# Second half of a fused attention and feed-forward kernel: the scheduler's order against program order on three engines

## The chip, the core and the metric

The kernel runs on one core of a Trainium2 chip. The core has a matrix engine (TensorE, here PE, with its weight loads shown apart as PEld), a vector engine (VectorE, DVE), an engine for functions of one element (ScalarE, ACT), a general engine (GpSimd, POOL) and SyncE (SP), which here only issues transfers. Each works through its own list of instructions in the order in which the built program holds it, and they meet through semaphores. The metric is the device time of the whole program in microseconds (us).

## The reference, cut to what matters

```python
attn = softmax(mask(q @ k.T / 8)) @ v            # 4 x 8 heads, 768 positions, window 128 and 4 sinks
x  = attn.reshape(3072, 512)
h  = np.maximum(x @ w_in, 0.0)                   # 512 -> 2048
x1 = h * h @ w_out                               # 2048 -> 512
a, b = x1 @ w1, x1 @ w2                          # 512 -> 1024, twice
out = (a * b @ w3) @ w_out2                      # 1024 -> 1024 -> 512, float32
```

## The kernel before, in words

The first half computes attention and the first feed-forward layer and writes most of `x1` to memory. Then `w3` and `w_out2` are folded into one matrix `w34` (`fold_T`, `fold_M`, L1193). What is left is the second half, on which the change works: per block of 512 tokens (six blocks, `order`, the loop after `pend = None`, L1555) and per slice `f` of 128 of the 1024 columns (eight slices), 48 passes in all. Every number is held as two float16 parts, high and low, so that one product is three matmuls for each of the two halves of its depth.

A pass is `ffn_C(n, f)` (L1291) and `ffn_D` (L1342). `ffn_C` gets `a` and `b` with a Strassen-like scheme: seven products of six matmuls each (128x128 weights, 256 columns), called P0 to P6 here after the first number in `prod(bx, 0, 0, True)`. They add up in three PSUM banks `bx`, `by`, `bz` (tile `cps`), taken in turn from four banks, so that the `by` of a pass is the `bx` of the pass before. Between the products of one bank stands a copy by ACT: s1 after P0, u2 after P4 (both into tile `cp`), u3 after P5 (tile `cq`). P4 may start when s1 is read, P5 when u2 is, P2 when u3 is. DVE adds c11 (tile `cq`, from s1 and P1), c22 (tile `cr`, from u3 and P3), c12 (tile `cr`, from u2 and P6), and multiplies twice into tile `asb`: s[0] after P2, s[1] after c12. Then `asb` is split into `h`: high part on ACT, low part on DVE. `ffn_D` is twelve matmuls of 512 columns with `h` as weights into four banks (tile `ops`), three for each bank; these run one pass behind, by `pend`.

Beside the passes stand: `upper` (ACT, tile `upj`), which sums squares for a range check, of each `h` and of some weights; `x1_ops` (L1251), which in a block prepares the operands `x1T` of the next one, with four subtractions on DVE (tile `x1t`) and seven splits, high part on ACT and low on DVE; `x1_load`, 1 MB from memory into `x1s`; and `ffn_out` (L1354), which at the end of a block reads the four `ops` banks, two on ACT and two on DVE, into `ost`, and sends it out, at the end of the program in four parts from SP and ACT by turns. `verdict` (L988) brings all range checks together on DVE into one number, which a one-column matmul `vps` sums and DVE turns into `flag`; every engine reads `flag` at the end and jumps over `general_path`, which does not run here.

Who sets the order: PE, ACT and DVE are wrapped in `InOrder` (L278). While `pinned[0]` is true, their instructions keep the order in which the code issues them. Otherwise a scheduler, which plans with times of its own, picks the order of each engine's list when the kernel is built. `pinned[0]` is true for most of the first half (L1488) and false from the last block of the first layer on, the second half included.

Of the kernel before, what the change touches and what calls it, by code (L numbers as in the profile page):

```python
# [14 lines left out]
ALU = mybir.AluOpType  # L15
# [281 lines left out]
def kernel(  # L297
# [17 lines left out]
    pinned = [False]  # L315
# [5 lines left out]
    KD, KF, K2 = DM // 128, DFF // 128, DF2 // 128  # L321
    BT = 512
    NB = NT // BT
    TB = BT // 128
# [41 lines left out]
    with ExitStack() as fast:  # L366
# [157 lines left out]
        def act_copy(out, in_, scale=1.0):  # L524
            ACT.activation(out=out, in_=in_, func=ACTF.Copy, scale=scale)
# [432 lines left out]
        def within(checks, name):  # L958

            n = sum(t.shape[1] * (t.shape[2] if len(t.shape) == 3 else 1) for t, _, _ in checks)  # L960
            inb = slab("t2", [128, n], F32, "inb", bufs=T2B)
            c0 = 0
            for t, bound, op in checks:
                n = t.shape[1] * (t.shape[2] if len(t.shape) == 3 else 1)
                d = inb[:, c0:c0 + n]
                if len(t.shape) == 3:
                    d = d.rearrange("p (a b) -> p a b", b=t.shape[2])
                DVE.tensor_scalar(out=d, in0=t, scalar1=bound, scalar2=None, op0=op)
                c0 += n
            low = top.tile([128, 1], F32, name=name)  # L970
            DVE.tensor_reduce(out=low, in_=inb[:, 0:c0], op=ALU.min, axis=AX.X)
            return low
# [12 lines left out]
            DVE.tensor_tensor(out=b, in0=b, in1=a, op=ALU.min)  # L985
            return b

        def verdict(low_att):  # L988

            low = within(  # L990
                ((st_w, W_MOST, ALU.is_lt), (st_w, W_LEAST, ALU.is_ge), (st_g, G_MOST, ALU.is_le)), "low_w"
            )
            up = within(((st_up, UP_MOST, ALU.is_le),), "low_up")
            DVE.tensor_tensor(out=low, in0=low, in1=up, op=ALU.min)
            DVE.tensor_tensor(out=low, in0=low, in1=low_att, op=ALU.min)

            DVE.scalar_tensor_tensor(out=low, in0=low, scalar=-1.0, in1=badf, op0=ALU.mult, op1=ALU.add)
            DVE.tensor_scalar(out=low, in0=low, scalar1=1.0, scalar2=None, op0=ALU.add)
            ps = bank("s0", "vps")
            PE.matmul(out=ps[0:1, 0:1], lhsT=low, rhs=ones, start=True, stop=True)  # L1000
            DVE.tensor_scalar(out=flag[0:1], in0=ps[0:1, 0:1], scalar1=0.5, scalar2=None, op0=ALU.is_ge)
# [289 lines left out]
        def ffn_C(n, f):  # L1291
# [23 lines left out]
            def add(out, a, ps):  # L1315
                DVE.tensor_tensor(out=out, in0=a, in1=ps, op=ALU.add)
# [3 lines left out]

            prod(bx, 0, 0, True)
            act_copy(s1, bx)
            prod(by, 3, 3, True)
            prod(bx, 4, 4, False)
            act_copy(u2, bx)
            prod(bz, 1, 1, True)
            add(c11, s1, bz)
            prod(bx, 5, 5, False)
            act_copy(u3, bx)
            add(c22, u3, by)  # L1330
# [4 lines left out]
            add(c12, u2, by)  # L1335
            mul(s[:, 1], c12, c22)
            h = slab("g", [128, 2, BT], F16, "h", bufs=GB)
            split(s.rearrange("p t c -> p (t c)"), h[:, 0], h[:, 1])
            h_t[n, f] = h
            yield  # L1340

        def ffn_D(n, f):  # L1342
            if f == 0:
                o_t[n] = [bank(f"b{c}", "ops") for c in range(TB)]
            h = h_t.pop((n, f))
            w = w34_t[f // 2]
            for t in range(TB):
                for i, (hp, wp) in enumerate(((0, 0), (0, 1), (1, 0))):
                    PE.matmul(
                        out=o_t[n][t], lhsT=h[:, hp, t * 128:(t + 1) * 128], rhs=w[:, wp, f % 2, :],  # L1350
                        start=(f == 0 and i == 0), stop=(f == K2 - 1 and i == 2),
                    )

        def ffn_out(n, k, last):  # L1354
            st = late_p[0].tile([128, TB, DM], F32, tag="ost", name="ost")
# [197 lines left out]
        rest = [w[0][:, c:d].rearrange("p a c f -> p (a c f)") for w in w12_t.values() for c, d in ((0, 4), (4, 7))]  # L1553
        rest += [w[:, 0].rearrange("p c f -> p (c f)") for w in w34_t.values()]
        pend = None  # L1555
        for o, n in enumerate(order):
            todo = []
            for f in range(K2):
                c = ffn_C(n, f)
                next(c)  # L1560
                if pend is not None:
                    ffn_D(*pend)
                next(c)
                if pend is not None and pend[1] == K2 - 1:
                    ffn_out(pend[0], o - 1, False)
                pend = (n, f)
                if f < 4:
                    upper(x1_t[n][0][:, 2 * f:min(7, 2 * f + 2)].rearrange("p a c f -> p (a c f)"))
                elif rest:
                    upper(rest.pop())  # L1570
                upper(h_t[n, f][:, 0])
                if f == 0 and o >= 1 and o + 1 < NB:
                    x1_load(o + 1)
                if f == 1 and o + 1 < NB:
                    x = x1s_t[o + 1]
                    todo = x1_ops(o + 1, x[:, 0:2], x[:, 2:4])
                for _ in range(2):
                    if todo:
                        todo.pop(0)()
        ffn_D(*pend)  # L1580
        assert not rest and ups[0] == NUP
        verdict(low_att)
        ffn_out(pend[0], NB - 1, True)

    gen = nc.values_load(flag[0:1, 0:1], min_val=0, max_val=1)
# [32 lines left out]
```

## Time and profile before

| what | us |
|---|---|
| three timed runs | 1108.42, 1110.32, 1110.94; median 1110.32 |
| the profiled execution, its own time | 1110.19 |
| its span on the core | 1108.0 |
| PE busy in the span | 1045.3 (94%) |
| DVE, ACT busy | 750.3 (68%), 709.4 (64%) |
| second half, first `cps` matmul to the end | 743.6 to 1108.0 |

Times in the trace count from the start of the span. A row of the timeline gives start, length, engine, operation, tile written and tiles read, and how many in a row; in brackets the idle time of the engine before it and what ended it. A PE row lasts until its last matmul's result is there, so rows that follow without a gap overlap by about 0.16.

### The profile page before, as it was taken

Reading aid. Unit: us, or ns where it says so; the run is one execution under the profiler, and the core shown is the slowest. Engines: PE = TensorE matmul, PEld = TensorE weight load, DVE = VectorE, ACT = ScalarE, POOL = GpSimd, SP = SyncE. Lnnn points to the kernel's source line nnn. Section 1 sums busy time; section 2 is a strip of 40 time slices with the busy share of each in tenths; the row PEclk is TensorE's granted clock in tenths of the full one; section 3 lists DMA queues with packets and bytes.
Section 4 is the critical chain, followed back from the end, with each engine's and each line's share of the span. In section 5 each row is a group of like instructions: output and inputs, shape, how many; then the busy total and the mean of one; then the engine's idle time right before and its main releaser. Section 6 shows DMA issues by size and latency. Waiting matters only on the chain. (4 is left out here: it accounts for less than half of the span.)

```text
span 1108.0 us, 20449 instructions
## 1 busy us (share of the span) xinstructions
PE 1045.3 (94%) x7146; PEld 636.4 (57%) x7146; DVE 750.3 (68%) x2292; ACT 709.4 (64%) x1836; POOL 45.0 (4%) x163
## 2 busy tenths in 40 slices
PE   6777897999999999999999998999999999999996
PEld 5665443555555555555554444457767776777774
DVE  8797888887788888877865667945363636453433
ACT  6975688887667666766754877854464546454532
POOL 2110111000000000000000000000000000000000
PEclk9867999999999999999999999999999999999998
DMA  8876787786567657556833324421020201010101
GB/s 189 157 157 140 179 204 184 150 183 122 104 144 145 117 107 173 118 114 144 147 68 99 115 96 140 164 75 40 2 77 1 77 1 39 1 39 1 38 1 41
DMA packets 265535, 113.46 MB, mean 102 GB/s; under 512 B 237648, under 2 KB 254032, under 8 KB 264784
## 3 DMA queue, kind: packets, MB, share of 16 engines
q1 hardware_dynamic: 265136, 111.55, 43.7%
q8 instruction: 58, 0.95, 0.4%
q14 instruction: 53, 0.43, 0.2%
q10 hardware_dynamic: 288, 0.52, 0.1%
HBM read 62.08 MB, written 11.53 MB: 66 GB/s over the span
## 5 line engine op out<-in xcount | busy, mean ns | idle before, releaser
L288 PE MATMUL hps<-xT,wi 128*128 128x512 f16 x1152 | 270.9, 386 | 0.0
L288 PE MATMUL x1ps<-g,wo 128*128 128x512 f16 x1152 | 265.6, 380 | 3.0 <-ACT g L288 2.0
L288 PE MATMUL cps<-x1T,w 128*128 128x256 f16 x2016 | 231.5, 273 | 7.2 <-DVE cq L288 4.6
L288 PEld LDWEIGHTS <-w 128*128 128x128 f16 x2016 | 196.9, 98 | 44.5 <-issue 9.1
L288 PEld LDWEIGHTS <-wi 128*128 128x128 f16 x1152 | 115.0, 100 | 123.2 <-issue 8.6
L288 PEld LDWEIGHTS <-wo 128*128 128x128 f16 x1152 | 109.8, 98 | 122.6 <-issue 5.7
L288 PE MATMUL ops<-w,h 128*128 128x512 f16 x576 | 133.5, 379 | 1.8 <-ACT h L288 1.8
L288 ACT ACTIVATE cp<-cps 128x256 f32<-128x256 f32 x96 | 36.1, 376 | 131.3 <-PE cps L288 131.3
L288 ACT ACTIVATE r<-hps 128x512 f32<-128x512 f32 x96 | 56.8, 592 | 94.7 <-PE hps L288 94.7
L288 ACT ACTIVATE pr<-pr,stt 128x264 f32<-128x264 f32 (+1 forms) x176 | 77.6, 483 | 32.9 <-DVE stt L288 31.5
L288 PEld LDWEIGHTS <-h 128*128 128x128 f16 x576 | 56.2, 98 | 58.1 <-ACT h L288 2.1
L288 DVE TENSOR_TENSOR ph<-pr,ph 128x512 f16<-128x512 f32 (+2 forms) x148 | 59.2, 436 | 35.2 <-ACT ph L288 33.2
L288 DVE SCALAR_TENSOR_TENSOR asb<-cq,cps 128x256 f32<-128x256 f32 x48 | 20.2, 420 | 87.6 <-PE cps L288 87.6
L288 DVE CUSTOM_DVE_ANT_0 pr<-sc,mask 128x264 f32<-128x264 f32 (+1 forms) x176 | 65.2, 400 | 16.1 <-PE sc L288 15.5
L288 PEld LDWEIGHTS <-pt 128*128 128x128 f16 x956 | 40.3, 98 | 34.5 <-issue 17.1
L288 ACT ACTIVATE ph<-pr 128x512 f16<-128x512 f32 (+2 forms) x148 | 55.9, 421 | 5.8 <-DMA pt<-ph 3.4
L288 ACT ACTIVATE g<-r 128x512 f16<-128x512 f32 x88 | 55.3, 629 | 2.4
L288 DVE TENSOR_TENSOR g<-r,g 128x512 f16<-128x512 f32 x56 | 38.6, 689 | 24.6 <-ACT g L288 24.4
L97 DVE SCALAR_TENSOR_TENSOR cvy<-cvy,cvt 128x512 int32<-128x512 int32 x72 | 49.1, 688 | 8.5 <-ACT cvy L86 8.3
L288 PE MATMUL y<-vp,pt 128*128 128x65 f16 (+1 forms) x888 | 40.6, 195 | 14.7 <-DVE xn L288 14.6
L288 DVE TENSOR_TENSOR h<-asb,h 128x512 f16<-128x512 f32 x48 | 33.2, 691 | 28.2 <-ACT h L288 28.2
L288 PEld LDWEIGHTS <-qT 128*128 128x128 f16 x592 | 41.4, 99 | 18.9 <-issue 0.7
(193 smaller groups left out, 1490.3 us busy)
## 6 DMA issues: line engine op xcount, KB each, us to landing
raw<-in_moe_w_out_dram SPq DMA_DIRECT2D x24, 512.0 KB
raw<-in_moe_w_dram SPq DMA_DIRECT2D x24, 512.0 KB
raw<-in_moe_w_in_dram SPq DMA_DIRECT2D x16, 512.0 KB
raw<-in_k_dram SPq DMA_DIRECT2D x84, 64.0 KB
raw<-in_q_dram SPq DMA_DIRECT2D x84, 64.0 KB
raw<-in_v_dram SPq DMA_DIRECT2D x84, 64.0 KB
x_dr<-x1e SPq DMA_DIRECT2D x20, 256.0 KB
x1s<-x_dr SPq DMA_DIRECT2D x5, 1024.0 KB
```

The source lines that it names most:

```text
L97: nc.vector.scalar_tensor_tensor(out=dst, in0=y, scalar=3, in1=t, op0=ALU.logical_shift_left, op1=ALU.bitwise_or)
L288: r = f(*args, **kw)
```

## The change

`pinned[0]` is set true ahead of the second half, so that PE, ACT and DVE run it as the code is written; SP isn't wrapped and is still planned. The code is written in another order for that. `ffn_C` hands over at two more places, after s1 and after c11, and the split of `asb` into `h` becomes a step of its own, `ffn_h`. A pass is now: P0, s1; split of the last pass's `h`; P3, P4, u2, P1, c11; `upper` of that `h`; P5, u3, c22; `ffn_D` of the last pass and, behind the last slice of a block, `ffn_out`; the load, two steps of `x1_ops`, the other `upper`; P2, s[0], P6, c12, s[1]. The last `ffn_D` may take the low parts of all four banks last (`i_outer`). The part of `verdict` that needs only old sums, with `low_att`, goes ahead of the last split as `verdict_w`.

```diff
+        def verdict_w(low_att):
             low = within(
                 ((st_w, W_MOST, ALU.is_lt), (st_w, W_LEAST, ALU.is_ge), (st_g, G_MOST, ALU.is_le)), "low_w"
             )
+            DVE.tensor_tensor(out=low, in0=low, in1=low_att, op=ALU.min)
+            return low
+
+        def verdict(low):
+
             up = within(((st_up, UP_MOST, ALU.is_le),), "low_up")
             DVE.tensor_tensor(out=low, in0=low, in1=up, op=ALU.min)
-            DVE.tensor_tensor(out=low, in0=low, in1=low_att, op=ALU.min)
...
             prod(bx, 0, 0, True)
             act_copy(s1, bx)
+            yield
             prod(by, 3, 3, True)
...
             add(c11, s1, bz)
+            yield
             prod(bx, 5, 5, False)
...
             h = slab("g", [128, 2, BT], F16, "h", bufs=GB)
-            split(s.rearrange("p t c -> p (t c)"), h[:, 0], h[:, 1])
+            h_t[n, f] = h, s.rearrange("p t c -> p (t c)")
+            yield
+
+        def ffn_h(n, f):
+            h, s = h_t[n, f]
+            split(s, h[:, 0], h[:, 1])
             h_t[n, f] = h
-            yield
-
-        def ffn_D(n, f):
+
+        def ffn_D(n, f, i_outer=False):
...
+            ti = [(t, i) for t in range(TB) for i in range(3)]
+            for t, i in sorted(ti, key=lambda x: x[1] == 2) if i_outer else ti:
...
         pend = None
+        pinned[0] = True
...
                 next(c)
                 if pend is not None:
+                    ffn_h(*pend)
+                next(c)
+                if pend is not None:
+                    upper(h_t[pend][:, 0])
+                next(c)
+                if pend is not None:
                     ffn_D(*pend)
...
+        low_w = verdict_w(low_att)
+        ffn_h(*pend)
+        upper(h_t[pend][:, 0])
+        ffn_D(*pend, i_outer=True)
+        assert ups[0] == NUP
+        verdict(low_w)
         ffn_out(pend[0], NB - 1, True)
```

PE, one pass in the middle of the first block, first matmul of each product alone (`x1T0` is the token operand, `cps_10185`, `cps_10186`, `cps_10187` are `bx`, `by`, `bz` of the pass, `cps_10105` and `cps_10106` those of the pass before it, `cps_10265` the next pass's `bx`; `ops` is `ffn_D`). Before:

```order
L288 MATMUL cps_10265<-x1T0_9374,w120_9039 128x256 [waits DVE_49]
...
L288 MATMUL cps_10105<-x1T0_9374,w12_7821 128x256 [waits Activation_49]
...
L288 MATMUL cps_10106<-x1T0_9374,w12_7821 128x256 [waits DVE_49]
...
L288 MATMUL cps_10185<-x1T0_9374,w120_8850 128x256 [waits Activation_49]
...
L288 MATMUL cps_10186<-x1T0_9374,w120_8850 128x256 [waits DVE_49]
...
L288 MATMUL cps_10187<-x1T0_9374,w120_8850 128x256 [waits DVE_49]
...
L288 MATMUL cps_10185<-x1T0_9374,w120_8850 128x256 [waits Activation_49]
...
L288 MATMUL ops_9977<-w34_9602,h_10174 128x512
```

These are P0 of the next pass, P2 and P6 of the last one, then P4, P3, P1, P5 of the pass, then `ffn_D`. The same pass now, whose banks are `cps_10181` to `cps_10183`:

```order
L288 MATMUL cps_10181<-x1T0_9374,w120_8850 128x256
...
L288 MATMUL cps_10182<-x1T0_9374,w120_8850 128x256 [waits DVE_49]
...
L288 MATMUL cps_10181<-x1T0_9374,w120_8850 128x256 [waits Activation_49]
...
L288 MATMUL cps_10183<-x1T0_9374,w120_8850 128x256 [waits DVE_49]
...
L288 MATMUL cps_10181<-x1T0_9374,w120_8850 128x256 [waits Activation_49]
...
L288 MATMUL ops_9977<-w34_9602,h_10180 128x512
...
L288 MATMUL cps_10181<-x1T0_9374,w120_8850 128x256 [waits Activation_49]
...
L288 MATMUL cps_10182<-x1T0_9374,w120_8850 128x256 [waits DVE_49]
```

That is P0, P3, P4, P1, P5, `ffn_D`, P2, P6: P0 has moved from a whole pass ahead to the head of its own pass, and one product instead of two stands between P4 and P5.

ACT, from the end of the first block's last whole pass on (`x1T0_10657` is the high part of the next block's operands). Before, and then the rows on the same operands now (`x1T0_9993`, prepared in the first block):

```order
L288 ACTIVATE cq_10421<-cps_10417 128x256
L288 ACTIVATE cp_10496<-cps_10493 128x256
L288 ACTIVATE x1T0_10657<-x1s_10575 128x512 x3
L288 ACTIVATE x1T0_10657<-x1t_10659 128x512 x2
L288 ACTIVATE x1T0_10657<-x1t_10660 128x512 x2
L288 ACTIVATE cp_10496<-cps_10493 128x256
```

```order
L288 ACTIVATE cq_10105<-cps_10101 128x256
L288 ACTIVATE x1T0_9993<-x1t_9995 128x512 x2
L288 ACTIVATE upj_10163,st_up_66<-x1T0_9374 128x512
L288 ACTIVATE cp_10184<-cps_10181 128x256
L288 ACTIVATE h_10180<-asb_10107 128x512
L288 ACTIVATE cp_10184<-cps_10181 128x256
```

Seven splits in a row between two copies have become one or two a pass, behind u3, with an `upper` behind them; and the split of `h` now stands between s1 and u2.

DVE, the end of the program, before and now:

```order
L288 TENSOR_REDUCE low_w_13687<-inb_13683 128x1
L288 SCALAR_TENSOR_TENSOR asb_13603<-cr_13602 128x256
L288 TENSOR_TENSOR h_13666<-asb_13603,h_13666 128x512
...
L288 TENSOR_SCALAR ost_13700<-ops_13186 128x512
L288 TENSOR_SCALAR ost_13700<-ops_13188 128x512
L288 TENSOR_SCALAR flag_63<-vps_13697 1x1
```

```order
L288 SCALAR_TENSOR_TENSOR asb_13599<-cr_13598 128x256
...
L288 TENSOR_REDUCE low_w_13671<-inb_13667 128x1
L288 TENSOR_TENSOR low_w_13671<-low_w_13671,low_att_8582 128x1
L288 TENSOR_TENSOR h_13666<-asb_13599,h_13666 128x512
...
L288 TENSOR_SCALAR flag_63<-vps_13697 1x1
L288 TENSOR_SCALAR ost_13700<-ops_13186 128x512
L288 TENSOR_SCALAR ost_13700<-ops_13188 128x512
```

The reduce has moved behind s[1], and `flag` ahead of the two reads of `ops`. On ACT the rows at the same place were `ost`, `ost`, two transfers, and are now by turns:

```order
L288 ACTIVATE ost_13700<-ops_13185 128x512
L288 DMA out_0_dram<-ost_13700 128x512
L288 ACTIVATE ost_13700<-ops_13187,cons_67 128x512
```

The first of these transfers sends what DVE writes into `ost`.

## Rows read from the trace of the kernel before

**Rows 1.** One stretch: length, then busy PE, PEld, DVE, ACT, POOL; clock; DMA.

```profile
991.10:1094.80 103.70, 103.70 (x776) 75.57 (x774) 40.43 (x90) 43.61 (x110) 0.00 (x0) 1.00 0.05 17
```

**Rows 2.** Timeline of PE: two groups of `ffn_D`, twelve passes apart.

```profile
998.29 2.75 PE L288 MATMUL ops<-w,h 128*128 128x512 f16 x12
...
1084.39 2.75 PE L288 MATMUL ops<-w,h 128*128 128x512 f16 x12
```

**Rows 3.** Timelines of PE, ACT and DVE at the end of the first block.

```profile
800.31 4.09 PE L288 MATMUL cps<-x1T,w 128*128 128x256 f16 x36
805.55 0.82 PE L288 MATMUL cps<-x1T,w 128*128 128x256 f16 x6 [1.14 <-DVE cq L288]
806.54 0.82 PE L288 MATMUL cps<-x1T,w 128*128 128x256 f16 x6 [0.18 <-ACT cp L288]
...
802.48 1.67 ACT L288 ACTIVATE x1T<-x1s 128x512 f16<-128x512 f32 x3 [3.14 <-PE cps L288]
...
803.28 1.89 DVE L288 TENSOR_TENSOR x1T<-x1s,x1T 128x512 f16<-128x512 f32 x3
805.08 0.41 DVE L288 TENSOR_TENSOR cq<-cp,cps 128x256 f32<-128x256 f32 x1
```

**Rows 4.** Instructions on the tile `cps`: shortest, median and longest, in ns.

```profile
L288 PE MATMUL cps<-x1T,w x2016: 269/273/273, 743.6 to 1094.7; 128*128 128x256 f16 x184
L288 ACT ACTIVATE cp<-cps x96: 359/378/385, 746.5 to 1089.1; 128x256 f32<-128x256 f32 x96
```

**Rows 5.** Timelines of PE and ACT: two hand-overs from PE through ACT to PE.

```profile
763.78 5.40 PE L288 MATMUL cps<-x1T,w 128*128 128x256 f16 x48
764.64 0.38 ACT L288 ACTIVATE cq<-cps 128x256 f32<-128x256 f32 x1 [2.47 <-PE cps L288]
...
746.53 0.37 ACT L288 ACTIVATE cp<-cps 128x256 f32<-128x256 f32 x1
746.95 0.81 PE L288 MATMUL cps<-x1T,w 128*128 128x256 f16 x6 [1.22 <-ACT cp L288]
```

**Rows 6.** Timelines of DVE and ACT in a pass without stall: s[1] and split.

```profile
795.76 0.42 DVE L288 SCALAR_TENSOR_TENSOR asb<-cr 128x256 f32<-128x256 f32 x1
796.24 0.62 ACT L288 ACTIVATE h<-asb 128x512 f16<-128x512 f32 x1
```

**Rows 7.** Groups of the second half: busy time, mean ns of one.

```profile
L288 DVE TENSOR_TENSOR x1t<-x1s 128x512 f32<-128x512 f32 x10 | 6.7, 686 | 3.5 <-DMA x1s<-x_dr 3.5
```

**Rows 8.** Timelines of PE, ACT and DVE where the second half begins.

```profile
735.41 8.37 PE L288 MATMUL w34ps<-wo,w3T 128*128 128x512 f16 x38
743.61 2.13 PE L288 MATMUL cps<-x1T,w 128*128 128x256 f16 x18
...
745.54 0.57 ACT L288 ACTIVATE w<-w34ps 128x512 f16<-128x512 f32 x1
...
748.26 0.68 DVE L288 SCALAR_TENSOR_TENSOR w<-w34ps,w 128x512 f16<-128x512 f32 x1
```

**Rows 9.** Timelines of PE, ACT and DVE at the end of the program.

```profile
1093.50 1.48 PE L288 MATMUL cps<-x1T,w 128*128 128x256 f16 x12
1096.80 2.76 PE L288 MATMUL ops<-w,h 128*128 128x512 f16 x12 [1.82 <-ACT h L288]
...
1096.12 0.63 ACT L288 ACTIVATE h<-asb 128x512 f16<-128x512 f32 x1 [4.62 <-DVE asb L288]
1099.90 0.94 ACTq L288 DMA_DIRECT2D out_dram<-ost  x2
...
1095.36 0.40 DVE L288 TENSOR_REDUCE low_w<-inb 128x1 f32<-128x240 f32 x1
1099.17 1.29 DVE L288 TENSOR_SCALAR ost<-ops 128x512 f32<-128x512 f32 x2 [0.34 <-PE ops L288]
1100.38 0.14 DVE L288 TENSOR_SCALAR flag<-vps 1x1 int32<-1x1 f32 x1
```

**Rows 10.** Queue instructions on the jump over `general_path`: count, ns, first start.

```profile
L1586 PEldq COMPARE_BRANCH x1: 4132/4132/4132, 1101.7 to 1101.7; - x1
```

More of the change, by code (lines that the diff above doesn't have):

```diff
@@ L986, in att_verdict @@
             return b
-        def verdict(low_att):
+        def verdict_w(low_att):
             low = within(
@@ L1346, in ffn_D @@
             w = w34_t[f // 2]
[L1347 to L1352, printed above, removed]
+            ti = [(t, i) for t in range(TB) for i in range(3)]
+            for t, i in sorted(ti, key=lambda x: x[1] == 2) if i_outer else ti:
+                hp, wp = ((0, 0), (0, 1), (1, 0))[i]
+                PE.matmul(
+                    out=o_t[n][t], lhsT=h[:, hp, t * 128:(t + 1) * 128], rhs=w[:, wp, f % 2, :],
+                    start=(f == 0 and i == 0), stop=(f == K2 - 1 and i == 2),
+                )
         def ffn_out(n, k, last):
@@ L1561 @@
                 if pend is not None:
-                    ffn_D(*pend)
[L1563 to L1571, printed above, removed]
+                    ffn_h(*pend)
[4 more added lines that the diff above has]
+                if pend is not None:
+                    ffn_D(*pend)
+                    if pend[1] == K2 - 1:
+                        ffn_out(pend[0], o - 1, False)
                 if f == 0 and o >= 1 and o + 1 < NB:
@@ L1579 @@
                         todo.pop(0)()
-        ffn_D(*pend)
-        assert not rest and ups[0] == NUP
-        verdict(low_att)
+                if f < 4:
+                    upper(x1_t[n][0][:, 2 * f:min(7, 2 * f + 2)].rearrange("p a c f -> p (a c f)"))
+                elif rest:
+                    upper(rest.pop())
+                next(c)
+                pend = (n, f)
+        assert not rest
+        low_w = verdict_w(low_att)
[4 more added lines that the diff above has]
+        verdict(low_w)
         ffn_out(pend[0], NB - 1, True)
```

## The prediction

> **What bounds the kernel now.** I read the stretches first. From 991 to 1095 us PE is busy for 103.70 of 103.70 us at a granted clock of 1.00, the full 2.4 GHz, while DVE and ACT are busy for some 40% of it [rows 1]: in the second half PE is the bound, and the two others matter only where they make it wait. So the question is how much of this half PE doesn't spend on issuing matmuls, and where.
>
> The length of a pass without a stall comes from two groups of ffn_D twelve passes apart: (1084.39 - 998.29) / 12 = 7.175 us [rows 2]. Forty-eight of them are 344.40 us. The half runs from its first matmul at 743.61 [rows 8] until the last matmul of the last ffn_D is issued. That group starts at 1096.80 and lasts 2.76, of which the last 0.16 is the way of the result into PSUM (a matmul of 256 columns lasts 0.273 and the next starts 0.109 after it, since 48 of them take 5.40 [rows 4, 5]): 1099.39. So the half takes 355.78 us, and 355.78 - 344.40 = **11.38 us are lost**. No order of the same matmuls gives back more than that.
>
> The loss stands in three places, in the timelines:
> - At block ends. ACT runs the seven splits for the next block in one go from 802.48, DVE follows with the low parts, and c11 comes after three of these, at 805.08 [rows 3]. PE has issued its 36 matmuls by 800.31 + 36 x 0.109 = 804.24 and goes on at 805.55, then again only at 806.54 instead of 806.21: 1.31 + 0.33, some 1.65 us. The pattern stands four times in the trace, so 6.6 us.
> - At the end: P6 is issued by 1093.50 + 1.48 - 0.16 = 1094.82, the last ffn_D starts at 1096.80, waiting for h [rows 9]: 1.98 us.
> - The rest, 11.38 - 6.6 - 1.98 = 2.8 us, at the beginning, where ACT splits operands of the second block before it serves the first products: w34's last part is read by ACT at 745.54, and DVE is done with it at 748.26 + 0.68 [rows 8].
>
> **The change part by part.**
>
> *The pass.* The work is the same; only the order differs. PE now runs P0, P3, P4, P1, P5, ffn_D, P2, P6. The hand-over s1 (P0 to P4) has one product, P3, as cover, where it had a whole pass; u2 (P4 to P5) has one, P1, where it had two; u3 (P5 to P2) has ffn_D. All depends on whether one product of 0.655 us (6 x 0.109) is enough. Counted from the start of the product's last matmul: 0.273 until it ends, some 0.04 until ACT starts (the sixth matmul of the run at 763.78 starts at 764.33, ends at 764.60, ACT starts at 764.64), 0.376 for the copy, 0.05 until PE goes on (copy over at 746.90, PE at 746.95): 0.74 us [rows 4, 5]. The cover, from the same point, is 0.109 + 0.655 = 0.764. That leaves 0.02 us. It is thin, but the trace shows this very case: the 48 matmuls from 763.78 hold P5, one product, P2, with the copy u3 between at 764.64, and 48 matmuls at 0.109 plus the tail make 5.40, what the row has. So no gap. I cost the hand-overs at 0, with 0.02 each as the upper end: two a pass, 95 of them, +1.9 us.
>
> What ACT does between them has to fit as well. With the end of P6 as zero, c12 and s[1] follow on DVE at 0.19 and 0.65; the split starts 0.48 after s[1] does, at 1.13, and takes 0.62 [rows 6], to 1.76. u2 is wanted at 3 x 0.655 + 0.19 = 2.16: 0.40 spare. The low part is ready at some 2.5, ffn_D wants it after P5 at 3.28. So a split between s1 and u2 costs nothing, as long as DVE isn't late.
>
> *Block ends.* The seven splits are spread over four passes, two in each, behind u3, where ffn_D covers them: two of 0.6 and an upper of 1.2 after u3, about 2.9 us after ffn_D's start, while the next s1 is wanted at 2.59 + 3 x 0.655 + 0.19 = 4.75. The 6.6 us go. In the one pass that has the four subtractions DVE is the tight engine: c22 ends about 1.0 after ffn_D's start, four subtractions and one low part of 0.69 each [rows 7] end at 4.4 (if none overlaps its neighbour) or 4.1 (two reads of ops take 1.29 together, so 0.6 from one to the next [rows 9]); then s[0] takes 0.42, and the next P3 may overwrite its bank at 4.6 to 4.9, and wants to at 4.555. That is 0.03 to 0.3 in each of five blocks; I take 0.05, so 0.25, with 0.1 and 1.5 as ends. ffn_out at a block's end reads the banks as they finish; the next ffn_D comes 7 products later, 4.6 us, so it hides. The loads on SP are issued a block ahead of use, and in the order now they still are.
>
> *Beginning.* P0 starts at 743.61 as before; P3 needs the bank of the last w34 product, which ends at 743.78. ACT, idle then, reads it by 744.4, DVE by 745.13 (0.57 and 0.68, [rows 8]), P3 at 745.18 where PE was free at 744.27: 0.91 stall. In the first pass there is no ffn_D, so P2 waits for u3 in full, 0.63. Together 1.54 instead of 2.8.
>
> *End.* The h of the last pass waits for c12, s[1] and the split as before. The reduce of 0.40 stood between c12 and s[1] [rows 9] and is now behind: 0.2 less (0 to 0.4), so 1.79 instead of 1.98. The last ffn_D had its low parts last already, so i_outer changes nothing.
>
> *Tail, from the last matmul to the end, 8.6 us.* flag no longer waits for DVE's two reads (1.29), so it is there 0.6 earlier; these reads come 0.6 later; and on ACT the second read now stands behind a transfer that waits for DVE's first one, so ACT reaches its own flag load some 0.65 later (its two transfers began at 1099.90 [rows 9]). The output's bytes end at about the same time, being held by bandwidth. Bounds -0.6 and +0.65; I take +0.3, since the later engine decides more of it. What ends the tail the rows leave open, the output's landing or the jump over general_path, which on PE lasts 4.13 us [rows 10].
>
> *The sum.* Lost now: 1.54 + 1.79 + 0.25 = 3.58, against 11.38: 7.80 us less; tail +0.3: 7.5 less. The profiled execution took 1110.19, the median is 1110.32, so they stand for each other: **1102.7 us**.
>
> **The rivals.**
> - *The hand-overs fall a little short.* Two a pass with 0.02 spare by modelled matmul ends. At 0.05 missing each, 95 x 0.05 = 4.8 us: 1107.5. For it: the longest copy is 0.385, and each wait now comes last. Against it: the run of 48 without a gap, which comes back in other blocks.
> - *They fall well short, slower than before.* The same place, s1 and u2, if PE's start after a wait that is really open costs more than rows show, say because ACT is held by the split of h whenever DVE is late. From 7.5 / 95 = 0.08 us each all is given back, from 0.1 it is slower; at 0.15 each, 14.3 us: 1117. Against it: the 0.40 spare above, and DVE's low load [rows 1].
> - *The stall at block ends changes its form.* If DVE's burst in one pass a block holds P3, and through s[1] the split and u2, for the 1.65 us that the old burst cost, 5 x 1.65 replace 6.6, and only beginning and end gain: 11.38 - 3.33 - 8.25 = -0.2, with the tail's 0.3 it is 0.5 more than before: 1110.7. Against it: 0.3 is the most that the durations make of it.
>
> - *The tail follows each engine's own jump.* If an engine needs some 4 us for the jump whatever the output does, ACT, the latest, sets the end: tail +0.65 instead of +0.3, 1103.0. PE's 4.13 us [rows 10] speak for it; that the output's landing isn't told apart from it in the rows, against. The Trainium skill (Runtime: NRT & Kernel Launch, section Instruction fetch mechanics) has this rule: a taken branch whose target isn't loaded stalls until its code is fetched. The length of PE's row agrees with it.
>
> **How the numbers follow.** The forecast gets 0.48, and the tail by the jump, which differs from it by 0.3 alone, 0.30, together 0.78; hand-overs a little short 0.12 (of it 0.02 so near that no change can be told); block ends in another form 0.04; well short 0.06. A measurement can tell about 0.2%, 2.2 us, from no change: the forecast, the tail's rival and most of the first rival lie below 1108.1, so faster 0.88; same 0.06; slower 0.06. Range: downwards burst and tail at their low ends give 1102.7 - 0.15 - 0.9 = 1101.7, and the runs of before reach 1.9 below their median, so 1100.3. Upwards burst 1.25, tail 0.35 and hand-overs 1.9 more: 1106.2.
>
> **What would show it.** PE's timeline of the second half as groups of 42 and 12 with no idle time behind ACT or DVE at block ends; ffn_D every 7.175 us; one gap of 0.9 before P3 at about 744.3 and one of 0.5 to 0.6 before P2 at 748; the last ffn_D starting near 1089, and the span ending near 1100.5. Wrong if the copies into cp show up as releasers of PE in every pass, or ffn_D comes later than 7.2 us after the last.

## The result and the profile after

The changed kernel takes 1099.4 us, median of four runs (1099.13 to 1101.41); the kernel before 1110.63 beside it. The ratio is 0.9899, 95% interval 0.9868 to 0.9929: faster by 11.2 us, and 3.3 below the predicted 1102.7. Direction and the mechanism of the second half are as predicted; the tail went the other way, and the time lies 0.9 under the range.

The profiled execution took 1101.41 at a span of 1099.2. The page, whose columns are busy time, share of the span and instructions, shows the same number of instructions as before on every engine. The span falls by 8.8, PE's busy time by 5.8, and DVE's rises by 7.9.

```profile
span 1099.2 us, 20433 instructions
...
PE 1039.5 (95%) x7146; PEld 635.0 (58%) x7146; DVE 758.2 (69%) x2292; ACT 711.0 (65%) x1836; POOL 47.9 (4%) x163
```

What [rows 1] showed for one good stretch now holds for nearly all of the second half. The view by stretches of after (length, busy PE, PEld, DVE, ACT, POOL, clock, DMA):

```profile
820.30:1086.00 265.70, 265.70 (x2003) 195.70 (x2001) 132.17 (x267) 133.03 (x321) 0.00 (x0) 1.00 0.07 25
```

PE's timeline of after at three places, the beginning, the end of the first block and the end of the program (start, length, engine, operation, count, and in brackets the idle time ahead and what ended it):

```profile
743.59 0.82 PE L288 MATMUL cps<-x1T,w 128*128 128x256 f16 x6
745.17 2.78 PE L288 MATMUL cps<-x1T,w 128*128 128x256 f16 x24 [0.76 <-DVE w L288]
748.42 4.74 PE L288 MATMUL cps<-x1T,w 128*128 128x256 f16 x42 [0.47 <-ACT cq L288]
753.00 2.75 PE L288 MATMUL ops<-w,h 128*128 128x512 f16 x12
...
798.64 4.75 PE L288 MATMUL cps<-x1T,w 128*128 128x256 f16 x42
803.23 2.75 PE L288 MATMUL ops<-w,h 128*128 128x512 f16 x12
805.82 4.75 PE L288 MATMUL cps<-x1T,w 128*128 128x256 f16 x42
...
1085.64 1.47 PE L288 MATMUL cps<-x1T,w 128*128 128x256 f16 x12
1088.75 2.76 PE L288 MATMUL ops<-w,h 128*128 128x512 f16 x12 [1.64 <-ACT h L288]
```

Where [rows 3] have 36, 6 and 6 matmuls with idle time in front, groups of 42 and 12 follow one another without any, across the block's end too. And these are all of PE's waits from 743 us to its end (who waits for whom, us in total, times, longest):

```profile
PE ops L288 <- ACT h L288: 1.6, 1, 1.6
PE cps L288 <- DVE w L288: 0.8, 1, 0.8
PE cps L288 <- ACT cq L288: 0.5, 1, 0.5
```

From here on, "second half" is the time from the first `cps` matmul to the issue of the last `ffn_D` matmul (its group's start + 2.59), and "tail" what follows until the span ends. Before, in the profiled execution: 355.78 and 8.61. After: 743.59 to 1088.75 + 2.59 = 1091.34, so 347.75, and 1099.2 - 1091.34 = 7.86. Both of these executions reach the second half at the same time (743.61 and 743.59), so their difference, 1110.19 - 1101.41 = 8.78, is all in these two: 8.03 + 0.75.

### The profile page after: what moved, and what is told of

It is laid out like the page before. It is cut to its first block, busy times and chain, and to the rows that moved or that the text cites. A ratio compares the mean times of both kernels' runs of the same rounds, so it can differ in the third digit from the quotient of the medians.

```text
span 1099.2 us, 20433 instructions
## 1 busy us (share of the span) xinstructions
PE 1039.5 (95%) x7146; PEld 635.0 (58%) x7146; DVE 758.2 (69%) x2292; ACT 711.0 (65%) x1836; POOL 47.9 (4%) x163
## 5 line engine op out<-in xcount | busy, mean ns | idle before, releaser
L288 PE MATMUL cps<-x1T,w 128*128 128x256 f16 x2016 | 228.2, 273 | 1.2 <-DVE w L288 0.8
```

What stands on the lines that cost most here:

```text
L288: r = f(*args, **kw)
```

## The experiments

Letters in the quoted expectations name the theories of that series; the text around them says them in words. The second half, the tail and the times stand together here (ratio to the kernel before on the same chip with its 95% interval, where there are several executions):

| kernel | second half | tail | median us | ratio |
|---|---|---|---|---|
| before | 355.78 | 8.61 | 1110.63 | |
| before_again | 357.09 | 8.45 | 1108.49 | 0.9991 (0.9975 to 1.0007) |
| before_look1, 2, 3 | 357.48, 355.75, 357.40 | 8.48, 8.50, 8.46 | one execution each | |
| unpinned | 355.87 | 8.48 | 1108.95 | 1.0002 (0.9988 to 1.0016) |
| after | 347.75 | 7.86 | 1099.4 | 0.9899 (0.9868 to 0.9929) |
| after_again | 347.75 | 8.08 | 1100.25 | 0.9903 (0.9880 to 0.9925) |
| after_third | 347.75 | 7.97 | 1099.33 | 0.9904 (0.9881 to 0.9927) |
| pin_only | 539.33 | 8.43 | one execution | |
| copy_twice | 374.75 | 7.89 | one execution | |
| x1_burst | 376.36 | 8.12 | one execution | |
| flag_last | 347.75 | 8.62 | 1101.16 | 0.9913 (0.9887 to 0.9940) |
| act_reads_first | 347.75 | 7.82 | 1098.66 | 0.9900 (0.9876 to 0.9923) |
| flag_early | 348.55 | 8.46 | one execution | |
| no_out | 347.75 | 6.27 | one execution | |
| out_half | 347.75 | 7.19 | one execution | |
| sp_sends | 347.74 | 7.82 | one execution | |
| best | 347.59 | 9.16 | 1099.95 | 0.9908 (0.9887 to 0.9928) |
| best4 | 347.37 | 7.33 | 1099.03 | 0.9904 (0.9880 to 0.9928) |

The last `ffn_D` of pin_only took 3.06 instead of 2.76, so its half is 0.3 longer, and its tail 0.3 shorter, than this rule has them.

### Is it the order, or the code?

**unpinned**: the new code, with the order left to the scheduler as before.

```diff
-        pinned[0] = True
         for o, n in enumerate(order):
```

> The new code without pinned[0] = True: the scheduler orders PE, ACT and DVE of the second half. The order that it builds has the seven splits in a row at four block ends again and P0 a pass ahead. Theory A (program order is what takes the bursts away; the new code order by itself does nothing): second half of 353 to 356 us with gaps of 1.1 us at four block ends, whole within 2 us of the kernel before. Rival (the new places of the splits and of ffn_h help under the scheduler too): second half of 348 to 351 us.

Nothing is gained: 355.87 and a ratio of 1.0002. PE's timeline of unpinned shows the stall of [rows 3] again, to the hundredth:

```profile
801.86 0.82 PE L288 MATMUL cps<-x1T,w 128*128 128x256 f16 x6 [1.14 <-DVE cq L288]
802.85 0.82 PE L288 MATMUL cps<-x1T,w 128*128 128x256 f16 x6 [0.18 <-ACT cp L288]
```

**pin_only**: the old code, in its own program order.

```diff
         pend = None
+        pinned[0] = True
         for o, n in enumerate(order):
```

> The old code with pinned[0] = True and nothing else: program order of the code before. There ACT has, behind the split of h, two sums of squares and two splits (4.3 us) ahead of the next s1, and h is split right after s[1], so P4 of the next pass waits for all of it. Theory A (the code had to be written in another order for program order to pay): 3 to 5 us of wait of PE for ACT in each of 48 passes, second half of 490 to 590 us. Rival (program order alone is what counts): second half of 347 to 352 us.

Its second half takes 539.33, that is 191.6 more than after, 4.0 a pass. Waits of the whole second half of pin_only, ACT's timeline in one pass, and PE in the whole stretch (length, busy PE, clock, DMA):

```profile
ACT h L288 <- DVE asb L288: 224.7, 48, 5.5
...
PE cps L288 <- ACT cp L288: 128.0, 47, 3.5
...
1003.27 0.63 ACT L288 ACTIVATE h<-asb 128x512 f16<-128x512 f32 x1 [4.43 <-DVE asb L288]
1003.80 0.83 ACT L288 ACTIVATE upj<-w 128x768 bf16<-128x768 f16 x1
...
1005.38 0.36 ACT L288 ACTIVATE cp<-cps 128x256 f32<-128x256 f32 x1
...
741.00:1281.00 540.00, 408.78 (x2594) 0.88 0.05 19
```

In the old code's order the split of `h` and two `upper` stand on ACT ahead of the next pass's s1, and PE waits for s1 in every pass, 128.0 us in all. Most of the other 63.6 goes with the clock: 0.88 on average, with PE busy for 408.78 where after has 344.84 at 1.00. So neither half of the change does it alone: the order has to be fixed, and the code has to hold an order worth fixing.

### Are the hand-overs as tight as the prediction said?

**copy_twice**: a second copy by ACT, into a tile of its own, ahead of s1 and of u2, so that each of the 95 hand-overs takes one ACT copy longer.

```diff
             prod(bx, 0, 0, True)
+            act_copy(twice(), bx)
             act_copy(s1, bx)
...
             prod(bx, 4, 4, False)
+            act_copy(twice(), bx)
             act_copy(u2, bx)
```

> The changed kernel with the copies s1 and u2 each made twice by ACT, the first time into a spare tile, so that P4 and P5 start when the second copy is done, 0.28 us later by ACT's rows (764.64 to 764.92). Theory A (each hand-over has 0.02 to 0.03 us to spare): 95 waits of 0.25 to 0.26 us, 24 to 25 us more in the second half, 371.5 to 372.5 us. Rival (the spare time is larger, since matmul ends are modelled): at 0.1 us to spare 17 us more, at 0.28 nothing.

27.0 us more, over 95 hand-overs 0.284 each. ACT's timeline has the two copies 0.28 apart, and PE's one of the gaps:

```profile
820.89 0.38 ACT L288 ACTIVATE twice<-cps 128x256 f32<-128x256 f32 x1 [0.42 <-PE cps L288]
821.17 0.38 ACT L288 ACTIVATE cp<-cps 128x256 f32<-128x256 f32 x1
...
821.60 0.81 PE L288 MATMUL cps<-x1T,w 128*128 128x256 f16 x6 [0.15 <-ACT cp L288]
```

All that is added on ACT comes out on PE: 0.28 in, 0.284 out. The spare time in a hand-over is 0 within what the rows resolve, a little under the 0.02 put down. The loss is 2 to 3 us above what was expected, since that had taken off 0.02 of spare time at each. So the kernel after has no slack that these rows could show in its 95 hand-overs, and still loses nothing in them: after's PE has no wait for `cp` in the list of waits above.

### Does the burst on DVE bite?

**x1_burst**: all steps of `x1_ops` in one pass of each block, as a burst, instead of two a pass.

```diff
-                for _ in range(2):
+                for _ in range(8):
```

> The changed kernel with all eight steps of x1_ops in the one pass with f = 1, so that the seven splits stand in a row on ACT and eleven operations on DVE, in program order. Theory A (spreading the steps over four passes is what makes block ends free): in five passes s[0] comes 3 to 3.6 us late, P3 of the next pass waits for it, 15 to 18 us more in the second half, 363 to 366 us, with five gaps of 3 to 3.6 us before a P3. Rival (PE has enough ahead): under 2 us more.

28.6 us more where 15 to 18 were expected. The waits have the expected size, 17.2 in all; the rest goes with the clock. PE's waits and the view by stretches of x1_burst around the second of the five gaps (last three numbers: clock, DMA share, GB/s):

```profile
PE cps L288 <- DVE asb L288: 17.2, 5, 3.4
...
815.00:820.00 5.00, 5.00 (x36) 1.00 0.22 81
820.00:825.00 5.00, 1.55 (x11) 0.82 0.52 179
825.00:830.00 5.00, 5.00 (x24) 0.50 0.08 31
```

PE stands for 3.45 us, and when it goes on, at 824.07, the granted clock is 0.50, 1.2 GHz instead of 2.4, until 830; 24 matmuls stand in these last 5 us, where the same length holds 36 at full clock. So a gap of 3.45 costs 5.7 on average (28.6 / 5), 5.2 to 6.5 one by one. A stall on a bound PE costs its own length only as long as the clock stays.

### What ends the tail?

The tail came out shorter by 0.75 where 0.3 more was put down. After `flag`, each engine loads it, jumps over `general_path` and signals. These are instructions of the engines' queues (count, shortest, median and longest ns, first and last start). ACT and SP of before:

```profile
L1585 ACTq TENSOR_LOAD <-flag x1: 1077/1077/1077, 1100.9 to 1100.9; - x1
...
L1586 ACTq COMPARE_BRANCH  x1: 54/54/54, 1102.0 to 1102.0; - x1
L1586 ACTq EVENT_SEMAPHORE  x1: 17/17/17, 1105.9 to 1105.9; - x1
...
L1586 SPq EVENT_SEMAPHORE  x8: 17/17/17, 1106.0 to 1106.6; - x8
```

and PE, ACT and SP of after:

```profile
L1605 PEldq TENSOR_LOAD <-flag x1: 488/488/488, 1091.9 to 1091.9; - x1
L1605 ACTq TENSOR_LOAD <-flag x1: 617/617/617, 1093.4 to 1093.4; - x1
...
L1606 SPq EVENT_SEMAPHORE  x8: 17/17/17, 1097.3 to 1097.8; - x8
...
L1606 SPq COMPARE_BRANCH  x1: 53/53/53, 1094.0 to 1094.0; - x1
L1606 ACTq COMPARE_BRANCH  x1: 54/54/54, 1094.1 to 1094.1; - x1
L1606 ACTq EVENT_SEMAPHORE  x1: 17/17/17, 1097.1 to 1097.1; - x1
```

From the branch to the semaphore behind it is the jump. Times behind `flag` count from the start of its writing (1100.38 before, 1091.67 after). Before, ACT loads `flag` 0.5 behind and jumps for 3.9. After, it loads it 1.7 behind, as predicted: its second transfer stands in front. But the load takes 0.62 instead of 1.08 and the jump 3.0 instead of 3.9, so ACT is through 5.4 behind `flag`, against 5.5 before. And `flag` itself comes 0.33 behind the last matmul's issue instead of 1.0. ACT isn't alone at the end: SP jumps from 1094.0 to 1097.3, and in both traces the last of its eight semaphores comes 1.4 us ahead of the end.

**flag_last**: `flag` behind DVE's two reads again, as before the change; all else as after.

```diff
-        verdict(low_w)
+        vps = verdict(low_w)
         ffn_out(pend[0], NB - 1, True)
+        set_flag(vps)
```

> The changed kernel with flag computed behind DVE's two reads of the last banks, as before the change. Theory A (the tail got shorter because flag is there before the output's bytes move, so that the engines load it in 0.5 us instead of 1.07 and jump earlier): the loads of flag take 1.0 to 1.1 us again, the tail is 8.3 to 8.6 us, the whole 0.5 to 0.7 us more than the changed kernel. Rival (the tail is set by the output's landing): DVE's reads 0.6 earlier, so the tail is 7.3 to 7.9 us, the whole the same or less.

The tail is back at 8.62, and PE's load of `flag` at 1058 ns. So moving `flag` ahead of the reads is what shortened it.

**act_reads_first**: ACT reads both its banks before its transfers.

```diff
                 else:
                     ACT.activation(out=st[:, t, :], in_=ps, func=ACTF.Copy, scale=scale)
-                if last:
+            if last:
+                for t in range(TB):
                     (SP, ACT)[t % 2].dma_start(out=dst[:, t], in_=st[:, t])
```

> The changed kernel with ACT's two reads of the last banks ahead of its two transfers, as before the change; flag stays first on DVE. If ACT, which reaches its jump last, sets the end, the tail shrinks by some 0.3 to 0.6 us to 7.3 to 7.6; if PE's jump after flag sets it, the tail stays at 7.8 to 7.9; if the landing of the output sets it, it shrinks by the time by which the last transfer is issued earlier, 0.3 to 0.7.

No gain: 7.82. ACT's transfers still wait for DVE's reads, so it loads `flag` 1.8 behind, as in after.

By then `flag` to the end was 7.5 to 7.8 us in all traces, with early and late loads. That could be a constant, or chance. The next runs tell it apart.

> The changed kernel once more, beside the three others of this series. Both theories: second half of 347.75 us from the first cps matmul to the last issue of ffn_D, tail behind it 7.8 to 8.1, flag to the end 7.5 to 7.8; the whole 1099 to 1101.5, since the first half varies by up to 4 us.

after_third, the changed kernel again, came as expected: 347.75 and 7.97.

**flag_early**: `flag` from the older checks alone, ahead of the last split.

```diff
-            up = within(((st_up, UP_MOST, ALU.is_le),), "low_up")
-            DVE.tensor_tensor(out=low, in0=low, in1=up, op=ALU.min)
...
         low_w = verdict_w(low_att)
+        verdict(low_w)
         ffn_h(*pend)
...
-        verdict(low_w)
         ffn_out(pend[0], NB - 1, True)
```

> Leaves the last upper out of the range check, so that flag can be set ahead of the last split and ffn_D. flag then stands 2 to 2.5 us ahead of the last matmul's issue instead of 0.33 behind it; the last ffn_D starts up to 0.6 later, as the check goes first on DVE and its one-column product first on PE. Theory A, the end follows flag by 7.5 to 7.8 us whatever else is queued: the tail behind the last matmul's issue falls from 7.9 to 5.0 to 5.5. Theory B, the end follows the engine that reaches its jump last, which is SP or ACT after their transfers of the output, some 2.7 us behind the last matmul's issue: the tail stays 7.7 to 8.1.

The tail is 8.46, with `flag` 2.5 us ahead of the last matmul's issue (written at 1087.55, issue at 1090.04): 10.9 from `flag` to the end, so it is no constant. The theory of the last jump, which put 7.7 to 8.1 down for this tail, missed as well. Here ACT and SP, which still have the sums to read and send, come to their jumps 4.9 and 4.5 behind `flag` and jump for 4.0 and 4.5.

**no_out**: the last block's output isn't sent.

```diff
-                if last:
-                    (SP, ACT)[t % 2].dma_start(out=dst[:, t], in_=st[:, t])
```

> Leaves out the four transfers of the last block's output; the sums are still read into ost. Theory A, the end follows flag by 7.5 to 7.8: the tail stays 7.8 to 8.1. Theory B, the end follows the engine that jumps last: SP and ACT now load flag with the others, some 0.2 behind it, jump at 0.8 instead of 2.3 behind it and, all engines together, need some 4.1 instead of 3.2: the tail falls to 7.1 to 7.4. If the bytes of the output itself held the end back, the tail would fall by more, to below 7.

The tail falls to 6.27, by more than the earlier entry of SP and ACT is worth. In no_out ACT's jump begins at 0.7 behind `flag` and takes 2.7:

```profile
L1604 ACTq COMPARE_BRANCH  x1: 50/50/50, 1092.6 to 1092.6; - x1
...
L1604 ACTq EVENT_SEMAPHORE  x1: 17/17/17, 1095.3 to 1095.3; - x1
```

**out_half**: two of the four transfers.

```diff
-                if last:
+                if last and t < 2:
```

> Leaves out two of the four transfers of the last block's output (one from SP and one from ACT stay). Theory D, the jumps wait for code that shares the transfer engines with the output's bytes: half of the bytes, half of what all four cost, so the tail stands between the 6.27 us without output and the 7.9 with it, at 6.9 to 7.3, and the jumps of ACT and SP at 2.8 to 3.2. Theory B, the latest entry plus a fixed jump: SP and ACT enter 0.2 to 1.5 earlier, jump 3.0 to 3.3, tail 6.5 to 7.7 by whichever is last. Told apart by the length of the jumps when the first bytes are over: D has them below 3.0 behind the bytes, B has 3.0 to 3.3.

7.19. Without output 6.27, with half of it 7.19, with all of it 7.9 to 8.1 (five traces whose end is as in after): some 0.9 for the first half MB and 0.7 to 0.9 for the second. The jump lengths don't follow as neatly: ACT's was 3.1, SP's 3.8 where 2.8 to 3.2 was expected.

**sp_sends**: SP sends all four parts, so that ACT is free at once.

```diff
-                    (SP, ACT)[t % 2].dma_start(out=dst[:, t], in_=st[:, t])
+                    SP.dma_start(out=dst[:, t], in_=st[:, t])
```

> All four transfers of the last block from SP; ACT sends nothing, so it loads flag with PE, DVE and POOL, some 0.2 behind flag, and SP enters its jump some 2.2 us behind the last matmul's issue instead of 2.7. Theory B, the latest entry plus a fixed jump of 3.0 to 3.3: the tail falls to 7.2 to 7.5. Theory D, the jumps wait for the output's bytes: ACT's jump, which now begins with the output in flight, grows from 3.0 to 4 or more, and the tail stays 7.7 to 8.5.

ACT's jump begins 0.7 behind `flag` instead of 2.4, and takes 3.9 instead of 3.0; the tail stays at 7.82:

```profile
L1606 ACTq COMPARE_BRANCH  x1: 50/50/50, 1089.0 to 1089.0; - x1
...
L1606 ACTq EVENT_SEMAPHORE  x1: 17/17/17, 1092.9 to 1092.9; - x1
```

SP came to its jump later than put down, 2.9 behind `flag`, and then needed only 2.7, so it was through at 5.6, as in after. With the same entry of ACT, the jump takes 2.7 without output and 3.9 with it in flight (one execution each; three traces of after have 3.0 to 3.2). The jumps of the other engines don't explain it: in no_out all five begin theirs within 0.3 us, in sp_sends all but SP. So a jump has no fixed length, as the theory of the latest entry wanted it: it is longer while the output moves, and an engine that comes to it 1.7 earlier gains 0.8 at its own end and nothing at the kernel's. The trace lists transfers of the kind "instruction" there, behind the last matmul, six and two on two queues in no_out as in after; they count on the same 16 DMA engines as the output's. The Trainium skill (Runtime: NRT & Kernel Launch, section Instruction fetch mechanics) says that a taken branch to code that isn't loaded stalls until it is fetched by DMA; the trace agrees. It shows besides that the jump takes 1.2 us longer while output is moving; whether the fetch itself grows, or a wait ahead of it, isn't shown.

### Two versions beyond the change

**best**: three small edits on the kernel after. The second pass's P0 stands where the first pass has no `ffn_D`; `vps` stands three matmuls ahead of the end; the output goes in two transfers.

```diff
+                else:
+                    ahead = ffn_C(n, f + 1)
+                    next(ahead)
...
-        ffn_D(*pend, i_outer=True)
-        verdict(low_w)
+        ffn_D(*pend, i_outer=True, mid=lambda: verdict(low_w))
...
-                if last:
-                    (SP, ACT)[t % 2].dma_start(out=dst[:, t], in_=st[:, t])
+            if last:
+                ACT.dma_start(out=dst[:, 0::2], in_=st[:, 0::2])
+                SP.dma_start(out=dst[:, 1::2], in_=st[:, 1::2])
```

> Three small edits on the changed kernel: the second pass's P0 stands in the place of the first pass's missing ffn_D, so that the 0.5 to 0.6 in front of the first P2 is covered (that pass's split then stands behind u2); the one-column product vps stands three matmuls ahead of the end of the last ffn_D, so flag comes 0.6 to 0.7 earlier; the output goes in two transfers, ACT's own two reads together and DVE's two from SP, so that SP and ACT are through with them 0.7 and 1.3 earlier. Both theories: second half 347.0 to 347.3 instead of 347.75, tail 7.1 to 7.4 instead of 7.9, together 1.1 to 1.3 us under the changed kernel of the same series. If neither flag nor the last jump is what ends the tail, only 0.5 to 0.7.

The tail is 9.16 instead of 7.2: the jumps of ACT and SP, which begin as the two transfers of 512 KB start to move, take 5.6 and 5.7. ACT's in best:

```profile
L1617 ACTq COMPARE_BRANCH  x1: 54/54/54, 1090.5 to 1090.5; - x1
...
L1617 ACTq EVENT_SEMAPHORE  x1: 17/17/17, 1096.1 to 1096.1; - x1
```

The second half gained only 0.16. The gap before P2 is gone, but a later split in the second pass pushes DVE back just where it has the four subtractions, and PE loses 0.22 there; and `vps` in the middle of `ffn_D` costs PE 0.23.

**best4**: four transfers again, and the second block's operands begun one pass later.

```diff
+                for t in range(TB):
+                    (SP, ACT)[t % 2].dma_start(out=dst[:, t], in_=st[:, t])
...
-                if f == 1 and o + 1 < NB:
+                if f == (1 if o else 2) and o + 1 < NB:
```

> The three small edits with two things changed: the output goes in four transfers again, from SP and ACT by turns behind the reads, and the operands of the second block are begun a pass later, away from the pass whose split stands behind u2. Both theories: second half 347.1 to 347.3 (0.5 to 0.6 under the changed kernel). Theory D: the tail stays with the output's bytes, 7.5 to 8.2, though flag comes 0.6 to 0.7 earlier; together 0.3 to 0.9 us under the changed kernel. Theory A, the tail follows flag: 7.1 to 7.3.

PE's timeline of best4, beginning and end:

```profile
742.40 0.82 PE L288 MATMUL cps<-x1T,w 128*128 128x256 f16 x6
743.97 7.38 PE L288 MATMUL cps<-x1T,w 128*128 128x256 f16 x66 [0.76 <-DVE w L288]
...
1088.98 0.19 PE L288 MATMUL vps<-cons,low_w 128*1 128x1 f32 x2
1089.11 0.82 PE L288 MATMUL ops<-w,h 128*128 128x512 f16 x3
```

From 743.97 on there are 66 matmuls where after has 24 and 42 with 0.47 between: that gap is covered. The last `ffn_D` starts 0.62 earlier against the first matmul than in after; 0.24 of it goes to `vps`. The tail is 7.33, between what each theory gave. From the first `cps` matmul to the end it is 354.7, against 355.6 to 355.8 in the three traces of the kernel after: 0.9 to 1.1 less. Whole times can't show so little: 1099.03 against 1099.33 to 1100.25.

### Where the rest of the gain is

The traces of the profiled pair show 8.78 us, the ratios 10.7 to 11.2. Repeats of both kernels were made for that.

> The changed kernel as it stands, a second time. Theory A (the order of the second half explains the gain: 8.0 us between the first product of the second half and the last ffn_D, and 0.75 us in the tail, as the two traces show; runs scatter by 2 us for another reason, in the first half): second half of 347.7 to 347.8 us again, tail of 7.8 to 7.9, and the start of the second half between 741 and 744 us. Ratio to before 0.990 to 0.992. Theory B (the 2 us by which three runs were quicker than the profiled one lie in the second half or the tail, so that the order brings more than the trace of one execution shows): the second half or the tail shorter by 1 to 2 us in a quicker execution.

> The kernel before, run as a kernel of its own, for its scatter and a second trace. Theory A: second half of 355.8 us again, tail of 8.6, and if the whole differs from 1108.0, the difference stands ahead of 743.6 us. Theory B: the difference stands in the second half.

after_again has the same second half to the hundredth. before_again has 357.09, 1.3 more than the profiled execution of before. Three more executions of the kernel before:

> The kernel before once more, for its second half alone. Theory F, the granted clock falls at the second half's beginning in a good part of its executions, as in one of three so far (0.91 from 740 to 760 us, 357.09 instead of 355.8): of three looks at least one shows it, which explains why whole times differ by 10 to 11 us and the traces of the second half and tail by 8.7. Rival: the halves measure 355.7 to 355.9 all three times, and what is left over is scatter of the first half.

> As the look ahead of it: 357.0 or more with a clock under 1.00 between 740 and 810 us by theory F, 355.7 to 355.9 by the rival.

> As the two looks ahead of it: 357.0 or more with a clock under 1.00 between 740 and 810 us by theory F, 355.7 to 355.9 by the rival.

Two of the three show it. PE's timeline of before_look3 where the second half begins, and its stretches there:

```profile
742.44 2.13 PE L288 MATMUL cps<-x1T,w 128*128 128x256 f16 x18
746.52 1.28 PE L288 MATMUL cps<-x1T,w 128*128 128x256 f16 x6 [1.95 <-ACT cp L288]
...
742.40:752.40 10.00, 7.58 (x55) 0.83 0.61 210
752.40:762.40 10.00, 10.00 (x78) 1.00 0.01 2
```

Behind the wait that [rows 5] show as 1.22, here 1.95, six matmuls take 1.28 instead of 0.81, and the clock over these 10 us is 0.83 on average. Three of five executions of before show this (waits of 1.32, 1.88 and 1.95; clock 0.83 in each), two don't (1.22 both times), nor does unpinned with its 1.28. None of the eight traces with after's order up to the last `ffn_D`, and its waits of 0.76 and 0.47, does: 347.74 or 347.75 each time. So the change takes away 1.3 to 1.7 us more in those executions, of which the longer wait itself is 0.1 to 0.7; why it is longer there isn't shown. The mean of before's five halves is 356.70, 8.95 above after, and with 0.53 of tail (8.50 against 7.97 on average) 9.5. That lies within all three intervals (7.9 to 14.7 us for after, 8.1 to 13.3 for the two others); the 1.2 to 1.7 us that are left to the ratios' 10.7 to 11.2 aren't settled.

The other part of the scatter isn't the change's at all. The first `cps` matmul comes anywhere between 739.85 and 743.83 us, with either kernel, though the code ahead of it is the same.

## Why the prediction was right in its mechanism and wrong in its range

- **Bound and loss.** Right. 355.78 - 344.40 = 11.38 were lost; 347.75 - 344.40 = 3.35 are now, and they stand where the prediction put them. P3 starts at 745.17, 0.92 behind the 744.25 at which PE was free (0.91 predicted); P2 waits 0.63, as predicted; the last `ffn_D` starts 1.80 behind P6's last issue (1.79).
- **Hand-overs at 0.** Right, and copy_twice shows how near it was: nothing is spare. The rivals in which they fall short didn't happen.
- **Block ends.** Right that the 6.6 go. The DVE burst, put down at 0.25 for five blocks, costs 0. Timelines of DVE and ACT of after in such a pass:

```profile
756.49 0.69 DVE L288 TENSOR_TENSOR x1T<-x1s,x1T 128x512 f16<-128x512 f32 x1
757.09 0.41 DVE L288 SCALAR_TENSOR_TENSOR asb<-cq,cps 128x256 f32<-128x256 f32 x1
...
757.87 0.42 DVE L288 SCALAR_TENSOR_TENSOR asb<-cr 128x256 f32<-128x256 f32 x1
...
758.33 0.63 ACT L288 ACTIVATE h<-asb 128x512 f16<-128x512 f32 x1 [0.19 <-DVE asb L288]
759.07 0.39 ACT L288 ACTIVATE cp<-cps 128x256 f32<-128x256 f32 x1
```

  The low part starts 0.60 ahead of s[0], so operations on DVE overlap, as in the better of the two cases weighed. s[0] is over at 757.50, and PE goes on without idle time. best shows the other side: with s[0] 4.32 behind `ffn_D`'s start instead of 4.09, the same pass costs 0.22.
- **Tail.** The step that failed: +0.3 predicted, -0.75 measured in the profiled pair (-0.53 on average). What the prediction named was there: behind the last matmul's issue, `flag` came 0.66 earlier (0.6 predicted), and ACT began its load at 2.1 instead of 1.5 (0.65 later predicted). The output's bytes, too, end at about the same time behind that issue, 4.2 before and 4.4 after, and while they move the 16 DMA engines are busy to a share of 0.6 to 1.05 in steps of half a microsecond. But the prediction carried ACT's delay on to the end, as if its load and its jump kept their lengths, and counted the earlier `flag` in the low end only. The load took 0.62 instead of 1.08 and the jump 3.0 instead of 3.9, so ACT was through 5.8 behind the last issue instead of 6.5. The rival in which the jump has a length of its own (+0.65) is out for the same reason. no_out and sp_sends show that the output in flight lengthens a jump; why after's is 0.9 shorter than before's, with the output in flight in both, stays open.
- **The range.** The second step that failed. Its low end doesn't add up as it stands: 1102.7 - 0.15 - 0.9 - 1.9 is 1099.75, not 1100.3. The measured 1099.4 is 0.35 below that too: 0.23 because 1.05 for the tail and 0.23 for the loss were due where 0.9 and 0.15 were allowed, and 0.12 because 1.9 was too little for the scatter. It came from three runs of before; 65 runs of it on record span 1105.79 to 1114.82.
- **The base.** That the profiled execution and the median stood for each other held for the kernel before alone. With the loss and the tail as the two traces have them, the base of 1110.19 gives 1101.42, which is the profiled execution of after (1101.41), by arithmetic; the other three took 1.9 to 2.3 less, with spans of 1096.9 to 1097.3. Both profiled executions came late to the second half (743.6, near the latest seen), and the one of before had its clock whole there, which not all have. That these two cancel in before is the likely reason, but argued: the other runs have no trace.

## What to carry to other kernels

A scheduler that plans with its own times can put a burst of work ahead of a hand-over that the bound engine waits for; where the bound engine's order is known, write the whole order out, code and lists together, and count each hand-over from the last instruction before it to the first behind it. Look at what a stall does to the clock behind it before pricing it at its own length. And ahead of a range, look at how far one and the same program spreads in stages that the change doesn't touch: a single profiled execution stands at one place in that spread.

## What the hardware showed that I had not expected

- A hand-over from PE through a copy of 256 columns on ACT and back is hidden by exactly one product of six matmuls: 95 of them with no wait, and 0.284 lost in each when ACT takes 0.28 longer.
- Behind a stand of 3.45 us PE ran at half its clock (24 matmuls in 4.4 to 5.3 us instead of 2.8), and in three of five executions of before it lost clock behind a wait of 1.3 to 1.95 us; those halves were 1.3 to 1.7 longer.
- The load of `flag`, a single number, took 0.46 to 0.55 us ahead of the output's first bytes, 1.03 to 1.13 just as these began to move (all engines of before, all but ACT of flag_last), and 0.52 to 0.80 on ACT in the midst of them.
- The jump over code that isn't run took 2.7 to 5.7 us on ACT and SP. On ACT it was 2.7 with no output, 3.9 where it began with the output (1 MB, four parts), 5.6 where that went in two parts. Why two parts cost so much more, and why flag_early's tail is longer than after's with the same transfers, stays open.
